# The maximum of v read by thirds, a last store from another tile, and a new load time in the planner

## The chip, the cores and the metric

The kernel runs on one core of one Trainium2 chip. The metric is the device time of one execution in microseconds. Each kernel is built once and run several times; the time before is the median of three runs. A profile is one further execution, recorded by the hardware profiler.

The engines are named as in the profile: PE is TensorE (matmuls), PEld its loads of the stationary operand, DVE is VectorE, ACT is ScalarE, POOL is GpSimd, SP is SyncE, on whose queue this kernel issues every DMA.

## The reference

Linear attention over 8 batches of 8 heads with 576 rows of 64, and then a feed-forward layer over the 4608 rows of 512 that come out of it:

```python
def phi(x):                                   # x: q or k
    proj = einsum('bhsd,df->bhsf', x, w_phi)  # 64 -> 128
    proj = proj - max(abs(proj), axis=-1, keepdims=True)
    return concatenate([exp(proj), exp(-proj)], axis=-1)
kv = einsum('bhsf,bhsd->bhfd', phi(k), v)
z = sum(phi(k), axis=2)
num = einsum('bhsf,bhfd->bhsd', phi(q), kv)
den = einsum('bhsf,bhf->bhs', phi(q), z)[..., None] + 1e-6
x = (num / den).transpose(0, 2, 1, 3).reshape(4608, 512)
h = x @ w_in                                  # 512 -> 2048
g = h / (1 + exp(-1.702 * h))
out = g @ w_out                               # 2048 -> 512
```

Inputs and output are float32; the two weights of the layer come as 64-bit floats.

## The kernel before

**Precision.** Most matmuls work on pairs of float16 or float32r numbers: a value is split into a high part and a low part, and three products are summed for one float32 product. To be split into float16, a tensor is scaled by a power of two that is taken from its maximum. For the attention's result that maximum is bounded by the maximum of |v| over a pair of batches (`SB = 2`). `batch_max(sb, stage)` (line 589) finds it for pair `sb`: it loads the whole of v of one batch into `stage`, 128 partitions by 2304 elements, reduces it on DVE to one column, does the same for the second batch, and `allmax` (line 533) carries the result across the partitions with a transpose and a matmul on PE. The four pairs are called pair 1 to pair 4 here (`sb` 0 to 3). The maximum gives `iv`, with which v is split, and `usc` and `osc`, with which the layer's intermediate values are scaled.

**Stages.** `load_weights` and `split_weights` bring the layer's weights in, turn them from 64-bit into float32 and split them; they share the first quarter of the span with the attention of the first two batches. From then on two kinds of work run interleaved: `attention(b)` for batches 2 to 7, and `moe_chunk`, the layer for 256 or 384 rows at a time. For each of 16 blocks `j` of 128 features `moe_chunk` runs a group of matmuls into one of two `hb` banks of PSUM; ACT takes the tanh of it (`th`), DVE makes `g` from `th` and the bank, which frees the bank; ACT and DVE split `g` into `gh` and `gl`; and matmuls over `gh` and `gl` add to the three `ab` banks. When a chunk is through, ACT copies each `ab` bank into one of two `osb` tiles, and `store` writes it out in one or two DMAs.

**Tiles.** A result of the attention for one batch lies in an `x` tile, of which there are three. `batch_max` uses as `stage` the `x` tile that its pair's first batch is going to fill. The weights that come in and `kept`, a partial result of the first two chunks, use `x` tiles too. `tl` is one tile of 128 partitions by 768 elements, in which `tail_load` (line 639) puts the last 64 rows of k, q and v of a batch. `e` is a pool of two tiles for exponentials.

**What sets the order.** Nothing is issued as it is written. A `Recorder` records every operation with its engine, tiles and dependencies; `R.part(v0, v1)` gives the operations behind it a due time between v0 and v1, in units of chunks of 384 rows. `schedule` (line 237) then plays a model of the engines: `cost` (line 192) gives each operation a duration, and of the operations that could start at an engine's free time the one with the earliest due time is taken; one that is due late is taken early if its engine has nothing else. A tile is handed to its next user when its last one is done. All operations are emitted in that order, each engine works through its own list in order, and semaphores keep the dependencies. So a changed duration, due time or tile changes the order on every engine. In the profile all these instructions carry one line, that of the recording, L346, and are told apart by tile names.

In `cost` a matmul has a load and a streaming time; a matmul may start, in the model, when the previous one has started and the load has passed:

```python
load = ap[1].shape[-1] / (1.2 if wide else 2.4)
...
return (load, n / 2.4 + (14.0 if wide else 3.0), 1)
```

`batch_max` of a pair is due at `u - VB`, where `u` is the due time of the pair's first batch (pair 1 has a due time of its own).

Of the kernel before, what the change touches and what calls it, by code (L numbers as in the profile page):

```python
# [8 lines left out]
F32 = mybir.dt.float32  # L9
# [101 lines left out]
class Recorder:  # L111
# [80 lines left out]
    def cost(eng, meth, args, kw):  # L192
# [9 lines left out]
        if eng == "tensor":  # L202

            wide = mybir.dt.size(ap[1].dtype) == 4
            load = ap[1].shape[-1] / (1.2 if wide else 2.4)
            if meth == "transpose":
                return (load, max(n, 32) / 2.4 * (2 if n > 64 else 1) + 1.5, 1)
            if ap[2].dtype == F32:
                m = 1.3 if n < 200 else 1.0
                return (m * load, m * n / 1.2, 2)  # L210
            return (load, n / 2.4 + (14.0 if wide else 3.0), 1)
# [138 lines left out]
def attn_moe_kernel(ctx, tc, q, k, v, w_phi, w_in, w_out, out):  # L350
# [10 lines left out]
    MAIN = 512  # L361
    TX = 0
    NEX = 6
# [43 lines left out]
    def new(nm):  # L407
        return R.tile(pools[nm])

    def small(n, nm="sm"):  # L410
        return R.tile(pools[nm])[:, 0:n]
# [176 lines left out]

    def batch_max(sb, stage):
        vmx = small(2, "sc")  # L590
        for i in range(2):
            R.sync.dma_start(
                stage,
                v[2 * sb + i].rearrange("h s d -> (h s d)").rearrange("(p n) -> p n", p=P),
            )
            R.vector.tensor_reduce(
                vmx[:, i : i + 1], stage, AX.X, ALU.max, apply_absolute_value=True
            )
        allmax(vg[:, sb : sb + 1], vmx)
        R.vector.reciprocal(iv[:, sb : sb + 1], vg[:, sb : sb + 1])  # L600
# [252 lines left out]

    def attn_unit(b, hp, nat, tail, nt, x32, x16, exact, bank):
        kq, vn = nat
# [133 lines left out]
        )  # L989
        j0 = 0  # L990
        xj = xf.rearrange("p j a d -> p j (a d)")
        if exact:
            tp = psa()
            for j in range(j0, 4):
                R.tensor.transpose(tp[:, j * P : (j + 1) * P], xj[:, j], ident)
            x, tp = slice(0, MAIN - j0 * P), tp[:, j0 * P :]
            R.scalar.copy(xh[:, hp, x], tp)
            R.vector.tensor_sub(xl[:, hp, x], tp, xh[:, hp, x])
        else:
# [67 lines left out]

    def moe_first(x32):

        acc = [R.tile(ab, whole=True) for m in range(TX // P)]  # L1070
        for j in range(NJ):
            R.part(-9.0 + 0.2 * j, -9.0 + 0.2 * (j + 1))
            load_weights(j)
            R.part(-5.825 + 0.54 * j, -5.825 + 0.54 * (j + 1), ("vector", "scalar"))
            hps = R.tile(hb, whole=True)[:, 0:TX]
            for ct in range(NCT):
                R.tensor.matmul(
                    hps,
                    wbuf[:, 2 * j + 1, ct * P : (ct + 1) * P],
                    x32[:, ct],  # L1080
                    start=ct == 0,
                    stop=ct == NCT - 1,
                )
            th = new("th")[:, 0:TX]
            R.scalar.activation(th, hps, AF.Tanh, scale=0.851)
            g = new("g")[:, 0:TX]
            R.vector.scalar_tensor_tensor(g, th, 1.0, hps, ALU.add, ALU.mult)
            for m in range(TX // P):
                R.tensor.matmul(
                    acc[m],  # L1090
                    g[:, m * P : (m + 1) * P],
                    wbuf[:, 2 * j + 2],
                    start=j == 0,
                    stop=j == NJ - 1,
                )
        for m in range(TX // P):
            osb = new("osb")
            R.scalar.activation(osb, acc[m], AF.Copy, scale=0.5)
            store(0, m * P, osb)

    def moe_chunk(sb, c0, n, part_=None):
# [35 lines left out]
        for m in range(n // P):  # L1137
            row = kept[:, c0 // P + m] if part_ is not None else None
            if part_ == 0:
                R.scalar.activation(row, acc[m], AF.Copy, scale=osf[:, 0:1])  # L1140
                continue
            osb = new("osb")
            if part_ is None:
# [8 lines left out]
    xs = {}  # L1152
    VB = 0.1
    V1 = (-1.1375, 0.5)
# [9 lines left out]
    def attention(b):  # L1164
        sb = b // SB
        u = v_att(4 * b)
        xt = new("x").rearrange("p t c s -> p (t c s)")
        x32, x16 = None, xt
        if b == 0 and TX:
            x32 = xt[:, 0 : 2 * NCT * TX].bitcast(F32).rearrange("p (c s) -> p c s", c=NCT)  # L1170
            x16 = xt[:, 2 * NCT * TX :]
        x16 = x16.rearrange("p (t c s) -> p t c s", t=2, c=NCT)
        xh, xl = x16[:, 0], x16[:, 1]
        xs[b] = (xh, xl)
        if b == 0:
            R.part(u + 0.002, u + 0.002)
            load_phi()
        R.part(u + 0.003 if b == 0 else u - 0.01, u)
        tl = tail_load(b)
# [5 lines left out]
        for hp in range(NHP):  # L1185
            if hp == 0 and b % SB == 0:
                z = u - VB if b else u + 0.975
                R.part(z, z)
                batch_max(sb, xt.bitcast(F32))
                if b == 0:  # L1190
                    R.vector.tensor_scalar(csx, vg[:, 0:1], 2.0**-13, None, ALU.mult)
            i = 4 * b + hp
# [5 lines left out]
            nat = attn_load(b, hp)  # L1198
            attn_unit(b, hp, nat, tail, nt, x32, x16, i < NEX, bank)
        return x32  # L1200

# [68 lines left out]
```

## Time and profile before

| | us |
|---|---|
| median of 3 runs | 1125.96 (1124.01 to 1129.14) |
| the profiled execution | 1123.7 |
| its span, first to last instruction | 1121.8 |
| PE busy in it | 1078.0 (96%) |
| PEld busy | 775.0 (69%) |
| DVE busy | 862.5 (77%) |
| ACT busy | 713.7 (64%) |
| POOL busy | 228.2 (20%) |

A busy PE is not PE at its peak, since the ends of matmuls are modelled and matmuls overlap; a PE that is idle is idle. The mean granted clock of TensorE over the span is 0.992 of full speed. Beside the page's shares the views that matter here are the busy time by stretch, the waits, and the timeline of PE and DVE around single waits.

### The profile page before, as it was taken

To read this page: it belongs to the slowest core of one execution; us is meant where nothing else is said; L and a number is where in the kernel's file an instruction comes from. 1 tells how busy PE (TensorE), PEld (TensorE's weight loads), DVE (VectorE), ACT (ScalarE), POOL (GpSimd) and SP (SyncE) were. 2 spreads that over 40 slices of the span, in tenths; PEclk is the share of its full clock that TensorE was granted. 3 is DMA by queue.
4 is the path that set the end of the run, shared out by engine and by line. 5 is a ranking of instruction groups with operands and counts; after the bars stand their busy time and mean duration, and the time that the engine had idled before them with its cause. 6 is when DMAs were issued, how large, how long until landed. Compare 5 with 4: busy or idle time off the path is not lost.

```text
span 1121.8 us, 22818 instructions
## 1 busy us (share of the span) xinstructions
PE 1078.0 (96%) x8915; PEld 775.0 (69%) x8915; DVE 862.5 (77%) x1763; ACT 713.7 (64%) x1483; POOL 228.2 (20%) x282
## 2 busy tenths in 40 slices
PE   5997999998999999999999999999999999999997
PEld 3664677876777757678876766678876667577653
DVE  5899988997799998887789988898879776422322
ACT  4577786874597876576677676586577666432423
POOL 6445101111123211230132211221122211100000
PEclk9998999999999999999999999999999999999999
DMA  8855113344143262242242252242223230000101
GB/s 271 267 183 143 57 38 78 73 97 144 23 94 77 61 179 48 53 97 56 48 100 57 58 162 57 61 105 58 48 67 58 42 63 11 11 29 2 29 1 29
DMA packets 172524, 87.80 MB, mean 78 GB/s; under 512 B 140032, under 2 KB 164736, under 8 KB 171392
## 3 DMA queue, kind: packets, MB, share of 16 engines
q1 hardware_dynamic: 172416, 86.34, 30.7%
q8 instruction: 70, 1.15, 0.4%
q14 instruction: 38, 0.31, 0.1%
HBM read 54.59 MB, written 9.44 MB: 57 GB/s over the span
## 4 chain that ended last, share of the span: by engine, by line
PE 77%; DVE 12%; ACT 5%; DMA 3%; issue 2%; SPq 1%; POOL 0%; ACTq 0%; DVEq 0%; POOLq 0%
PE ab L346 30%; PE hb L346 28%; PE at L346 19%; DMA xT<-xs 2%; DVE el L346 2%; DVE sm L346 2%; DVE t L346 1%; ACT e L346 1%; DVE gl L346 1%; DVE g L346 1%; DVE ks L346 1%; ACT eh L346 1%; DVE sc L346 1%; DVE vs L346 1%; DVE xs L346 1%
## 5 line engine op out<-in xcount | busy, mean ns | idle before, releaser
L346 PE MATMUL hb<-x,wbuf 128*128 128x192 f16 (+3 forms) x3264 | 479.8, 281 | 6.2 <-DVE g L346 5.9
L346 PE MATMUL ab<-wbuf,gh 128*128 128x512 f16 x1152 | 345.2, 382 | 0.2
L346 PEld LDWEIGHTS <-wbuf 128*128 128x128 f16 x3264 | 280.4, 98 | 80.5 <-issue 8.4
L346 ACT ACTIVATE th<-hb,usc 128x384 f32<-128x384 f32 (+1 forms) x208 | 115.8, 557 | 136.8 <-PE hb L346 126.6
L346 PE MATMUL ab<-wbuf,gl 128*128 128x512 f16 x576 | 198.8, 382 | 1.1 <-DVE gl L346 1.0
L346 DVE SCALAR_TENSOR_TENSOR g<-th,hb 128x384 f32<-128x384 f32 (+1 forms) x208 | 107.3, 517 | 105.6 <-ACT th L346 103.5
L346 PEld LDWEIGHTS <-gh 128*128 128x128 f16 x1152 | 108.9, 98 | 80.3 <-ACT gh L346 2.2
L346 DVE TENSOR_TENSOR el<-e,eh 128x512 f16<-128x512 f32 (+1 forms) x210 | 145.9, 708 | 18.8 <-PE at L346 9.3
L346 DVE SCALAR_TENSOR_TENSOR gl<-g,al,gh 128x384 f16<-128x384 f32 (+1 forms) x176 | 111.5, 635 | 37.2 <-ACT gh L346 30.5
L346 ACT ACTIVATE gh<-g,al 128x384 f16<-128x384 f32 (+1 forms) x176 | 106.9, 609 | 50.9 <-DVE g L346 50.2
L346 POOL TENSOR_TENSOR xf<-nf,rc 128x512 f32<-128x512 f32 x28 | 31.3, 1118 | 422.1 <-DVE rc L346 309.6
L346 DVE TENSOR_REDUCE sm<-at 128x4 f32<-128x512 f32 x126 | 86.1, 683 | 21.3 <-PE at L346 20.6
L346 PE MATMUL at<-ph,xT 128*128 128x128 f16 x944 | 98.7, 222 | 0.3
L346 ACT ACTIVATE e<-at 128x512 f32<-128x512 f32 x144 | 85.7, 604 | 20.7 <-PE at L346 19.3
L346 ACT ACTIVATE e<-t 128x512 f32<-128x512 f32 x144 | 89.4, 637 | 5.5 <-DVE t L346 3.7
L346 PEld LDWEIGHTS <-gl 128*128 128x128 f16 x576 | 54.6, 98 | 50.4 <-DVE gl L346 7.2
L346 DVE SCALAR_TENSOR_TENSOR t<-at,ks,sm 128x512 f32<-128x512 f32 x118 | 87.8, 744 | 1.2
L346 PE MATMUL at<-kzs,eh 128*128 128x132 f32 x216 | 79.8, 376 | 0.0
L346 PE MATMUL at<-vs,eh 128*128 128x132 f32 x208 | 79.5, 382 | 0.0
L346 PEld LDWEIGHTS <-xT 128*128 128x128 f16 x944 | 67.1, 99 | 13.9 <-issue 0.5
L346 PE MATMUL at<-kzs,el 128*128 128x66 f32 (+1 forms) x212 | 73.3, 351 | 0.0
L346 PE MATMUL at<-vs,el 128*128 128x66 f32 x208 | 73.3, 352 | 0.0
(195 smaller groups left out, 1926.4 us busy)
## 6 DMA issues: line engine op xcount, KB each, us to landing
x<-in_v_dram SPq DMA_DIRECT2D x8, 1152.0 KB, 6.4
vn<-in_v_dram SPq DMA_DIRECT2D x64, 128.0 KB, 2.8
kq<-in_k_dram SPq DMA_DIRECT2D x32, 256.0 KB, 3.1
kq<-in_q_dram SPq DMA_DIRECT2D x32, 256.0 KB, 3.0
x<-in_moe_w_in_dram SPq DMA_DIRECT2D x10, 512.0 KB, 5.4
x<-in_moe_w_out_dram SPq DMA_DIRECT2D x10, 512.0 KB, 5.2
out_dram<-osb SPq DMA_DIRECT2D x40, 128.0 KB, 2.6
out_dram<-osb SPq DMA_DIRECT2D x16, 256.0 KB, 2.4
```

Of the source, the lines that this page charges most:

```text
L346: f(*[g(a) for a in o.args], **{k: g(a) for k, a in o.kw.items()})
```

## The change

- `batch_max` for pairs 2 to 4 reads each batch in three loads of 768 elements per partition into the `tl` tile and reduces each third to a column of its own; `allmax` then reduces six columns in place of two. Pair 1 still uses its `x` tile.
- It is recorded ahead of `tail_load`, so its thirds come before the pair's first tail in the one `tl` tile; it no longer holds an `x` tile; `VB` goes from 0.1 to 0.5, which makes it due earlier.
- The last block of output that the kernel copies goes into an `e` tile and not into an `osb` tile.
- In `cost` the load of a 16-bit operand is counted at 4.6 columns per ns in place of 2.4: 28 ns for 128 columns in place of 53.
- `moe_first`, `TX`, `x32` and `j0` are removed; with `TX = 0` none of them did anything.

```diff
-            load = ap[1].shape[-1] / (1.2 if wide else 2.4)
+            load = ap[1].shape[-1] / (1.2 if wide else 4.6)
...
-    def batch_max(sb, stage):
-        vmx = small(2, "sc")
-        for i in range(2):
-            R.sync.dma_start(
-                stage,
-                v[2 * sb + i].rearrange("h s d -> (h s d)").rearrange("(p n) -> p n", p=P),
-            )
+    def batch_max(sb, stage=None):
+        n = 1 if stage is not None else 3
+        vmx = small(SB * n, "sc")
+        for i in range(SB * n):
+            t = stage if n == 1 else new("tl").rearrange("p i s d -> p (i s d)")
+            vr = v[SB * sb + i // n].rearrange("h s d -> (h s d)").rearrange(
+                "(p a n) -> p a n", p=P, a=n
+            )
+            R.sync.dma_start(t, vr[:, i % n])
             R.vector.tensor_reduce(
-                vmx[:, i : i + 1], stage, AX.X, ALU.max, apply_absolute_value=True
+                vmx[:, i : i + 1], t, AX.X, ALU.max, apply_absolute_value=True
             )
...
-            osb = new("osb")
+            if c0 + n == SB * S and sb == B // SB - 1 and m == n // P - 1:
+                osb = new("e")[:, 0:DM]
+            else:
+                osb = new("osb")
...
-    VB = 0.1
+    VB = 0.5
...
+        if b % SB == 0:
+            z = u - VB if b else u + 0.975
+            R.part(z, z)
+            batch_max(sb, None if b else xt.bitcast(F32)[:, 0 : H * S * D // P])
+            if b == 0:
+                R.vector.tensor_scalar(csx, vg[:, 0:1], 2.0**-13, None, ALU.mult)
         R.part(u + 0.003 if b == 0 else u - 0.01, u)
         tl = tail_load(b)
...
         for hp in range(NHP):
-            if hp == 0 and b % SB == 0:
-                z = u - VB if b else u + 0.975
-                R.part(z, z)
-                batch_max(sb, xt.bitcast(F32))
-                if b == 0:
-                    R.vector.tensor_scalar(csx, vg[:, 0:1], 2.0**-13, None, ALU.mult)
```

The order that comes of it, at three places.

DVE at the maximum of pair 3. In the kernel before, the reduction of a whole batch (`sc` from `x`) stands directly ahead of the `g` of two groups:

```order
L346 TENSOR_SCALAR ks_78<-ks_83,phg_163 128x2
L346 TENSOR_REDUCE sc_134<-x_113 128x1
L346 SCALAR_TENSOR_TENSOR g_117<-th_115,hb_65 128x384
L346 TENSOR_TENSOR el_144<-e_93,eh_141 128x512
L346 SCALAR_TENSOR_TENSOR g_118<-th_116,hb_64 128x384
```

In the changed kernel the first two thirds of this pair (`sc` from `tl`) stand so:

```order
L346 TENSOR_REDUCE sc_134<-tl_88 128x1
L346 SCALAR_TENSOR_TENSOR t_90<-at_62,ks_76,sm_126 128x512
L346 SCALAR_TENSOR_TENSOR xs_73<-kq_70,ks_77,xs_73 128x8x64
L346 TENSOR_SCALAR ks_86<-ks_86 128x2
L346 RECIPROCAL ks_81<-ks_86 128x2
L346 TENSOR_SCALAR ks_79<-ks_86,phg_163 128x2
L346 TENSOR_TENSOR el_144<-e_93,eh_142 128x512
L346 SCALAR_TENSOR_TENSOR g_117<-th_115,hb_65 128x384
L346 TENSOR_REDUCE sc_134<-tl_88 128x1
```

One reduction of 2304 elements has become three of 768, with seven other instructions between the first two of them.

SP at the same maximum. Before, the two loads of whole batches (`x` from v) have transposes and stores between them:

```order
L346 DMA x_113<-in_v_dram 128x2304
L346 DMA_TRANSPOSE xT_74<-xs_72 128x8x128
L346 DMA out_dram<-osb_123 64x512 x2
L346 DMA out_dram<-osb_124 64x512 x2
L346 DMA_TRANSPOSE xT_75<-xs_73 128x8x128
L346 DMA x_113<-in_v_dram 128x2304
```

Now:

```order
L346 DMA tl_88<-in_v_dram 128x768
L346 DMA_TRANSPOSE xT_75<-xs_73 128x8x128
L346 DMA tl_88<-in_v_dram 128x768 x3
L346 DMA_TRANSPOSE xT_75<-xs_72 128x8x128
L346 DMA_TRANSPOSE xT_74<-xs_73 128x8x128
L346 DMA tl_88<-in_v_dram 128x768
L346 DMA_TRANSPOSE x_114<-xo_111 128x4x128 x2
L346 DMA kq_70<-in_k_dram 128x2x256
L346 DMA kq_70<-in_q_dram 128x2x256
L346 DMA tl_88<-in_v_dram 128x768
```

Two loads have become six, three of them in a row, and two transposes of `xs` stand behind these three.

ACT at the end of the program, before (`ab` banks copied into `osb` tiles 124, 123 and 124 again):

```order
L346 ACTIVATE th_116<-hb_64,usc_176 128x384
L346 ACTIVATE gh_120<-g_118,al_172 128x384
L346 ACTIVATE osb_124<-ab_66,osc_177 128x512
L346 ACTIVATE osb_123<-ab_68,osc_177 128x512
L346 ACTIVATE osb_124<-ab_67,osc_177 128x512
```

and now:

```order
L346 ACTIVATE th_116<-hb_64,usc_176 128x384
L346 ACTIVATE gh_120<-g_118,al_172 128x384
L346 ACTIVATE osb_124<-ab_66,osc_177 128x512
L346 ACTIVATE osb_123<-ab_68,osc_177 128x512
L346 ACTIVATE e_93<-ab_67,osc_177 128x512
```

The last one writes a tile that no store reads.

## Rows read from the trace of the kernel before

**Rows 1.** The page, its first part: busy us, share of the span, instructions.
```profile
PE 1078.0 (96%) x8915; PEld 775.0 (69%) x8915; DVE 862.5 (77%) x1763; ACT 713.7 (64%) x1483; POOL 228.2 (20%) x282
```

**Rows 2.** Busy time by stretch: stretch, length, each engine, clock, DMA share, GB/s.
```profile
116.00:250.00 134.00, 132.86 (x1095) 98.00 (x1094) 120.83 (x272) 103.84 (x228) 18.89 (x24) 1.00 0.27 61
116.00:1114.00 998.00, 983.54 (x8364) 710.73 (x8362) 766.97 (x1589) 640.20 (x1342) 164.87 (x216) 1.00 0.27 62
490.00:500.00 10.00, 8.06 (x82) 7.54 (x81) 7.83 (x19) 5.87 (x13) 0.07 (x1) 0.83 0.22 54
```

**Rows 3.** Waits: who for whom, us in total, times, longest us.
```profile
PE hb L346 <- DVE g L346: 5.9, 6, 1.8
...
DVE sc L346 <- DMA x<-in_v_dram: 4.2, 3, 1.8
```

**Rows 4.** Instructions on tile sc: count, ns min/median/max, first and last start.
```profile
L346 DVE TENSOR_REDUCE sc<-x x8: 2536/2549/2553, 30.0 to 671.4; 128x1 f32<-128x2304 f32 x8
...
L346 DVE TENSOR_REDUCE sc<-sc x4: 99/143/148, 57.2 to 674.1; 128x1 f32<-128x2 f32 x4
```

**Rows 5.** Timeline, pair 2: start, us, engine, instruction, [idle before it <-releaser].
```profile
260.61 2.55 DVE L346 TENSOR_REDUCE sc<-x 128x1 f32<-128x2304 f32 x1 [1.82 <-DMA x<-in_v_dram]
263.08 0.74 DVE L346 SCALAR_TENSOR_TENSOR g<-th,hb 128x256 f32<-128x256 f32 x2
...
263.55 1.00 PE L346 MATMUL hb<-x,wbuf 128*128 128x64 f16 x18 [1.85 <-DVE g L346]
...
277.10 1.58 DVE L346 SCALAR_TENSOR_TENSOR vts<-tl,iv,vt 64x256 fp32r<-64x256 f32 x2
278.72 0.75 DVE L346 SCALAR_TENSOR_TENSOR g<-th,hb 128x256 f32<-128x256 f32 x2
...
279.19 0.39 PE L346 MATMUL hb<-x,wbuf 128*128 128x64 f16 x8 [0.92 <-DVE g L346]
```

**Rows 6.** Timeline, pairs 3 and 4.
```profile
404.27 2.55 DVE L346 TENSOR_REDUCE sc<-x 128x1 f32<-128x2304 f32 x1 [0.79 <-DMA x<-in_v_dram]
...
407.34 0.97 PE L346 MATMUL hb<-x,wbuf 128*128 128x384 f16 x5 [1.59 <-DVE g L346]
...
415.03 2.54 DVE L346 TENSOR_REDUCE sc<-x 128x1 f32<-128x2304 f32 x1
...
418.09 0.97 PE L346 MATMUL hb<-x,wbuf 128*128 128x384 f16 x5 [0.73 <-DVE g L346]
...
671.42 2.55 DVE L346 TENSOR_REDUCE sc<-x 128x1 f32<-128x2304 f32 x1 [1.58 <-DMA x<-in_v_dram]
...
674.39 0.27 PE L346 MATMUL at<-ident,sc 128*1 128x128 f32 x1 [1.19 <-DVE sc L346]
```

**Rows 7.** DMA issues of the page: count, KB each, median us to landing.
```profile
x<-in_v_dram SPq DMA_DIRECT2D x8, 1152.0 KB, 6.4
...
kq<-in_k_dram SPq DMA_DIRECT2D x32, 256.0 KB, 3.1
...
x<-in_moe_w_in_dram SPq DMA_DIRECT2D x10, 512.0 KB, 5.4
x<-in_moe_w_out_dram SPq DMA_DIRECT2D x10, 512.0 KB, 5.2
```

**Rows 8.** Matmuls of 64 columns: timeline; group by shape (busy us, mean ns, idle before).
```profile
250.20 0.51 PE L346 MATMUL hb<-x,wbuf 128*128 128x64 f16 x12
...
L346 PE MATMUL hb<-x,wbuf 128*128 128x64 f16 x192 | 9.4, 193 | 3.1 <-DVE g L346 3.0
```

**Rows 9.** Timeline of the end: PE, ACT and SP.
```profile
1113.95 0.38 PE L346 MATMUL ab<-wbuf,gl 128*128 128x512 f16 x1
...
1113.51 1.27 ACT L346 ACTIVATE osb<-ab,osc 128x512 f32<-128x512 f32 x2 [1.35 <-PE ab L346]
...
1116.02 0.59 SPq L346 DMA_DIRECT2D out_dram<-osb  x1
...
1117.31 0.69 ACT L346 ACTIVATE osb<-ab,osc 128x512 f32<-128x512 f32 x1 [2.54 <-DMA out_dram<-osb]
```

More of the change, by code (lines that the diff above doesn't have):

```diff
@@ L361, in attn_moe_kernel @@
     MAIN = 512
-    TX = 0
     NEX = 6
@@ L852, in across, with attn_unit @@
             R.scalar.copy(dst, tp.rearrange("p (j d) -> p j d", j=4))
-    def attn_unit(b, hp, nat, tail, nt, x32, x16, exact, bank):
+    def attn_unit(b, hp, nat, tail, nt, x16, exact, bank):
         kq, vn = nat
@@ L989, in attn_unit @@
         )
-        j0 = 0
         xj = xf.rearrange("p j a d -> p j (a d)")
@@ L993, in attn_unit @@
             tp = psa()
-            for j in range(j0, 4):
+            for j in range(4):
                 R.tensor.transpose(tp[:, j * P : (j + 1) * P], xj[:, j], ident)
-            x, tp = slice(0, MAIN - j0 * P), tp[:, j0 * P :]
-            R.scalar.copy(xh[:, hp, x], tp)
-            R.vector.tensor_sub(xl[:, hp, x], tp, xh[:, hp, x])
+            R.scalar.copy(xh[:, hp, 0:MAIN], tp)
+            R.vector.tensor_sub(xl[:, hp, 0:MAIN], tp, xh[:, hp, 0:MAIN])
         else:
@@ L1065, in store @@
             p0 += n
[L1068 to L1082, printed above, removed]
-                )
[L1084 to L1096, printed above, removed]
-            osb = new("osb")
-            R.scalar.activation(osb, acc[m], AF.Copy, scale=0.5)
-            store(0, m * P, osb)
     def moe_chunk(sb, c0, n, part_=None):
@@ L1141, in moe_chunk @@
                 continue
-            osb = new("osb")
+            if c0 + n == SB * S and sb == B // SB - 1 and m == n // P - 1:
+                osb = new("e")[:, 0:DM]
+            else:
+                osb = new("osb")
             if part_ is None:
@@ L1167, in attention @@
         xt = new("x").rearrange("p t c s -> p (t c s)")
[L1168 to L1172, printed above, removed]
+        x16 = xt.rearrange("p (t c s) -> p t c s", t=2, c=NCT)
         xh, xl = x16[:, 0], x16[:, 1]
@@ L1198, in attention @@
             nat = attn_load(b, hp)
-            attn_unit(b, hp, nat, tail, nt, x32, x16, i < NEX, bank)
-        return x32
+            attn_unit(b, hp, nat, tail, nt, x16, i < NEX, bank)
     attention(0)
```

## The prediction

> **What bounds the kernel now.** I read the page's busy shares first, then busy time by stretch, then the waits, then the timeline around the longest waits of TensorE. TensorE is busy for 96% of the span [rows 1], and from 116 to 1114 us it is busy 983.54 of 998 us [rows 2]. So in nine tenths of the span the time is set by how many matmuls stand there, which the change leaves alone, and a change of order can win only the 14.5 us that TensorE idles there, the end behind the last matmul, and what a low clock costs. VectorE (DVE) is the engine that TensorE waits for: 120.83 busy of 134 us between 116 and 250 [rows 2], and "hb <- DVE g" is the longest kind of wait of TensorE in the steady part, 5.9 us in 6 waits [rows 3].
>
> These waits have one origin more often than any other. The maximum of v over a pair of batches reads one whole batch per reduction: 8 reductions of 128x2304, 2.55 us each [rows 4], two in a row per pair. DVE takes its instructions in order, so the `g` that frees a bank of `hb` stands behind them. At 260.61 DVE starts such a reduction, after 1.82 us of waiting for the load; `g` follows at 263.08, and TensorE has idled 1.85 us when it gets the bank at 263.55 [rows 5]. After the second one, `g` at 278.72 stands behind the scaling of v by this maximum (vts), and TensorE idles 0.92 us [rows 5]. The next pair costs 1.59 and 0.73 us at 407.34 and 418.09, the last one 1.19 us at 674.39, where a matmul takes the reduction's own result [rows 6]. Together 1.85 + 0.92 + 1.59 + 0.73 + 1.19 = 6.3 of the 14.5 us. The other 8.2 us are many waits without a common cause. The first pair's two reductions stay as they are.
>
> **Part 1: maxima by thirds, sooner.** For pairs 2 to 4 the change takes out 6 loads of 1152 KB and 6 reductions of 2.55 us, and puts in 18 loads of 384 KB and 18 reductions of 768 elements. One takes 0.85 (a third of 2.55) to 0.94 us (with the 0.14 us of a reduction of two elements [rows 4] not shared out); I take 0.9. DVE work goes from 15.3 to 16.2 us: +0.9 us, on an engine with idle time. The gain is in the size of the piece. The slack between DVE and TensorE can be read off the waits: a delay of 1.82 + 2.55 cost 1.85 (slack 2.5), 0.79 + 2.55 cost 1.59 (1.75), 2.55 alone cost 0.73 (1.8) [rows 5, 6]. Against the smallest slack, 1.75 us, a third of 0.9 us alone costs TensorE nothing.
>
> The price: all thirds use the one `tl` tile. The next load waits on SyncE's queue (SP) until DVE has reduced the one before, and what is queued behind it there waits too: loads of k and q, transposes xT and x. A load of 384 KB does not occur before. 256 KB land in 3.1 us, 512 KB in 5.2 to 5.4, 1152 KB in 6.4 [rows 7]; the line from 256 to 1152 KB gives 3.5 (estimate), the 512 KB rows, taken while the weights came in, bound it at 5.3. I take 3.5, since 256 KB is nearest and the weights are in by then. Between the ends of the 15 successions the order leaves DVE other work, which I summed with the durations of the trace: 3.6, 3.8, 1.9, 9.6, 4.8 us in pair 2; 3.4, 4.3, 2.7, 17.9, 10.5 in pair 3; 3.1, 20, 5.9, 5.0, 8.5 in pair 4. Where it is under 3.5 us, DVE waits for the load: 1.6, 0.1, 0.8 and 0.4 us. Each with its 0.9 us, less the slack of 1.75: 0.8 us of TensorE once, else nothing. At a landing of 5.3 the same working gives 8.8 us. So part 1 is 0.8 - 6.3 = -5.5 us, with ends at -6.3 and +2.5. Of the 1.19 us at 674.39, which is the chain behind the last reduction and not its length, I leave 1 us standing: -4.5 us. If a stall goes, next late is `g` behind other DVE work, which is where the 8.2 us come from.
>
> Here a rule speaks against the change. The rows say 6.4 us for a whole batch and 3 x 3.5 = 10.5 us for its thirds. The Trainium skill (DMA: Bandwidth & Descriptors, "Measured (HBM→SBUF, 128 partitions, SWDGE, issued from GpSimd)") advises loads of 1 MiB or more, and its section "Anatomy of one DMA — SWDGE (gpsimd) path" gives 2.0 us plus bytes at 436 KB per us: 2.9 us for a third, 4.7 for the whole, an estimate by that page. By it the whole sum below would be about -7.9 in place of -7.3, since thirds would be awaited less; the trace's 6.4 us for 1152 KB is longer than the page's, and the trace decides.
>
> **Part 2: where they are put.** With VB 0.5, and no `x` tile to wait for, pair 2's reductions move from 260 us to the stretch that held 139 to 168 us, where the weights are split. DVE idles 13.2 us between 116 and 250 [rows 2], which covers 6 x 0.9 = 5.4 us; without that cover they would cost 5.4. The scaling by the maximum then no longer stands in front of `g` as at 277.10.
>
> **Part 3: last block from an `e` tile.** The last activation waits 2.54 us for its `osb` tile, whose store is under way [rows 9]. With its own tile it starts behind the two before it (they end at 1114.78, the last matmul at 1114.33) and ends near 1115.5. But SP issues the stores one after the other, and the fourth ends at 1116.61 [rows 9], so the fifth starts there, near 1116.7, and not at 1118.0, where the last activation ends now. -1.3 us, and nothing can take it back; ends -1.0 and -2.5 (the whole wait).
>
> **Part 4: the shorter float16 load.** No instruction changes; the planner counts 28 ns in place of 53 for a load of 128 columns. Twelve matmuls of 64 columns, each with its own load, take 0.51 us, the last one's 0.19 among it: 29 ns apart [rows 8]. So the new figure is the true one, and the plan's time for DVE against TensorE comes nearer the chip. Its effect is a new order everywhere after 98 us. One thing can be counted: the TensorE work between the end of a group in a bank of `hb` and the next group in this bank (spaced as in the trace). It must cover tanh and `g`. It is under 1.5 us at 7 places before, at 2 now. The unattributed 8.2 us, and a stretch of 10 us at a mean granted clock of 0.83 between 490 and 500 [rows 2], so 1.7 us lost to the lower level of 1.2 GHz behind two waits of TensorE, are what this can act on. I take -1.5 us, ends -6 and +5: a new order also makes new waits.
>
> **Sum.** -4.5 - 1.3 - 1.5 = -7.3 us on the profiled execution's 1123.7 (span 1121.8): 1116.4. The median of the runs shown, 1125.96, lies 2.3 above that execution, so the forecast for a median is 1118.7.
>
> **Rivals.** (a) The order is better throughout: nearly all of 6.3 us, 5 of the 8.2 and the 1.7 of the clock go: -5.5 - 1.3 - 6.7 = -13.5, 1112.5. For it: 7 places against 2. Against: pair 2's attention work is drawn forward into a stretch where DVE is already 90% busy. (b) The wait is exchanged: DVE awaits thirds as it now awaits whole batches (4.2 us in 3 waits [rows 3]), part 1 and part 4 are nothing, the end's 1.3 us stay: 1124.7. (c) Slower: SP's queue. In pairs 3 and 4 three thirds stand in a row with xT transposes directly behind. If a third lands in 5.3 us and not 3.5, each moves the transposes by 1.8 us, 5.4 per pair, 10.8 in all, with part 1 at +2.5 and the end at -1.3: +12, 1138. It decides from a landing of about 4.2 us on. Against it: 256 KB land in 3.1. (d) The plan's new figure is too short and its order denser than the chip can follow: half of the 8.2 us comes on top, +4.1 - 4.5 - 1.3 = -1.7, 1124.3; the 29 ns speak against it. Beside it stands the Trainium skill (TensorE: Matmul & The Clock Gate, "LDWEIGHTS (loading the stationary operand)"): columns / 1.2 ns, 107 ns for 128 columns; by that rule (d) would be the likeliest, but the trace does not agree with it.
>
> **How the numbers follow.** About 0.5% (5.6 us) is what a measurement here can tell from no change: faster is under 1120.3, slower over 1131.6. The forecast has 0.58, with its own range of 1114 to 1123: 0.44 of it faster, 0.14 the same. (a) 0.13, faster. (b) 0.13 and (d) 0.06, the same. (c) 0.10, slower. That is 0.57, 0.33 and 0.10. The range reaches from 1110 (all lower ends: -6.3 - 2 - 6, and a little for the runs) to 1128, which takes in (b), (d) and the milder part of (c).
>
> **What would show it.** Right: 18 reductions of about 0.9 us and none of 2.55 behind 60 us; thirds landing in 3 to 4 us; "hb <- DVE g" at a third of its 5.9 us; the last activation without a wait. Wrong: DVE waits for `tl` loads above 5 us in sum; TensorE waits for xT behind them; TensorE idle above 14 us between 116 us and the last matmul, or a new stretch at the lower clock.

## Result and profile after

The changed kernel takes 1111.42 us, median of 6 runs (1108.15 to 1112.23); the kernel before, run beside it, 1126.11 (1124.01 to 1129.14). The ratio is 0.9862, with a 95% interval of [0.9841, 0.9882]: 14.7 us faster. The direction was forecast and the size was not: 7.3 us were expected. The profiled execution took 1108.6 us, its span is 1106.8 (before 1121.8).

The page of the changed kernel, busy time first, then three of the costliest groups and the loads of thirds:

```profile
PE 1071.5 (97%) x8915; PEld 772.9 (70%) x8915; DVE 857.5 (77%) x1775; ACT 713.4 (64%) x1483; POOL 225.9 (20%) x282
...
L346 PE MATMUL hb<-x,wbuf 128*128 128x192 f16 (+3 forms) x3264 | 480.4, 281 | 1.4 <-DVE g L346 1.3
L346 PE MATMUL ab<-wbuf,gh 128*128 128x512 f16 x1152 | 342.0, 382 | 3.0 <-ACT gh L346 3.0
...
tl<-in_v_dram SPq DMA_DIRECT2D x18, 384.0 KB, 3.2
```

Against [rows 1], TensorE does the same 8915 matmuls in 6.5 us less busy time. The rest of the span, in which it isn't busy, goes from 43.8 to 35.3 us. So of the 15.0 us, 8.5 are idle time and 6.5 are time that the page of before called busy. The same by stretch, changed kernel, columns as in [rows 2]:

```profile
116.00:250.00 134.00, 133.96 (x1113) 99.61 (x1111) 125.73 (x284) 104.29 (x231) 24.47 (x33) 1.00 0.35 80
116.00:1099.00 983.00, 976.58 (x8364) 708.38 (x8363) 762.40 (x1600) 639.89 (x1341) 158.68 (x215) 1.00 0.29 63
490.00:500.00 10.00, 9.96 (x98) 7.87 (x97) 9.97 (x20) 6.19 (x14) 1.49 (x3) 1.00 0.43 110
```

From 116 us on, as many matmuls as in [rows 2], 8364, stand in 983 us and not in 998: 8.0 us less idle (14.46 before, 6.42 now), 7.0 us less busy. Between 490 and 500 us the granted clock is at its upper level (2.4 GHz) throughout, where it was 0.83 on average. The 1.7 us that the lower level cost there [rows 2] can be part of the 7.0; the other 5.3 us have another cause.

The waits of TensorE in the changed kernel, and the thirds of the maximum as DVE works through them:

```profile
PE ab L346 <- ACT gh L346: 3.0, 6, 0.8
...
PE hb L346 <- DVE g L346: 1.3, 3, 0.8
```

```profile
L346 DVE TENSOR_REDUCE sc<-tl x18: 900/944/954, 140.8 to 625.7; 128x1 f32<-128x768 f32 x18
```

"hb <- DVE g" is down from 5.9 us in 6 waits [rows 3] to 1.3 in 3. A wait of `ab` for ACT's `gh` has come up instead, 3.0 us. Every sign that the prediction named for being right is there (18 reductions near 0.9 us, thirds landing in 3.2 us, this wait below a third, the last activation without a wait), and none of those for being wrong. The signs didn't tell that the sum was wrong; the experiments did.

### The profile page after: what moved, and what is told of

The parts are those of the page before. It is cut to its first block, busy times and chain, and to the rows that moved or that the text cites. A ratio compares the mean times of both kernels' runs of the same rounds, so it can differ in the third digit from the quotient of the medians.

```text
span 1106.8 us, 22847 instructions
## 1 busy us (share of the span) xinstructions
PE 1071.5 (97%) x8915; PEld 772.9 (70%) x8915; DVE 857.5 (77%) x1775; ACT 713.4 (64%) x1483; POOL 225.9 (20%) x282
## 4 chain that ended last, share of the span: by engine, by line
PE 86%; DVE 5%; ACT 4%; DMA 2%; issue 1%; SPq 1%; POOL 0%; ACTq 0%; DVEq 0%; POOLq 0%
PE ab L346 33%; PE hb L346 31%; PE at L346 21%; DMA xT<-xs 2%; ACT e L346 1%; SPq L346 1%; DVE sm L346 1%; DVE ks L346 1%; ACT eh L346 0%; DVE gl L346 0%; DMA kq<-in_q_dram 0%; DVE t L346 0%; DVE wbuf L346 0%; DVE vs L346 0%; DVE g L346 0%
## 5 line engine op out<-in xcount | busy, mean ns | idle before, releaser
L346 PE MATMUL ab<-wbuf,gl 128*128 128x512 f16 x576 | 195.2, 382 | 0.4 <-DVE gl L346 0.3
L346 PE MATMUL at<-ph,xT 128*128 128x128 f16 x944 | 105.4, 222 | 0.5 <-DVE t L346 0.5
```

The source lines that it names most:

```text
L346: f(*[g(a) for a in o.args], **{k: g(a) for k, a in o.kw.items()})
```

## Experiments: the parts, one by one

All runs of an experiment stand against runs of the kernel before on the same chip, in 3 rounds (5 for the last pair); the ratio is to these. Their medians lay between 1124.1 and 1126.1 us over all sessions.

**The `e` tile alone.**

```diff
-            osb = new("osb")
+            if c0 + n == SB * S and sb == B // SB - 1 and m == n // P - 1:
+                osb = new("e")[:, 0:DM]
+            else:
+                osb = new("osb")
```

> The kernel before with one edit: the last copied block of output goes into an e tile. If the end is a term of its own, -1.3 us (ratio 0.9988), the last activation no longer waits 2.54 us, and the rest of the order stays as it was. If the end's gain is taken back elsewhere (the stores behind each other on SP), under -0.5 us.

Measured 1123.63, ratio 0.9990 [0.9974, 1.0006]. The last activation no longer waits, as [rows 9] let one expect (ACT at the end, this kernel):

```profile
1115.28 1.27 ACT L346 ACTIVATE osb<-ab,osc 128x512 f32<-128x512 f32 x2 [1.35 <-PE ab L346]
1116.43 0.69 ACT L346 ACTIVATE e<-ab,osc 128x512 f32<-128x512 f32 x1
```

Every instruction of TensorE and of DVE stands in the same order as before, so this is no new order. The size agrees with -1.3 us, but the interval holds no change too. The profiles are sharper than the runs: from the end of the last matmul to the end of the span it is 7.5 us before (1114.33 [rows 9] to 1121.8) and 6.3 us here (1116.10 to 1122.4).

```profile
1115.72 0.38 PE L346 MATMUL ab<-wbuf,gl 128*128 128x512 f16 x1
```

In all six kernels of this study with the `e` tile this stretch is 6.3 or 6.4 us, in the fourteen without it 7.5 to 7.7. So the tile is worth some 1.2 us at the end, though the times of the runs scatter too much to show it.

**The load figure alone.**

```diff
-            load = ap[1].shape[-1] / (1.2 if wide else 2.4)
+            load = ap[1].shape[-1] / (1.2 if wide else 4.6)
```

> The kernel before with one edit: the planner counts the load of a 16-bit operand at 4.6 columns per ns. Theory L (a plan nearer to the chip makes a denser order of matmuls): TensorE's busy time falls by most of the 6.5 us by which it fell in the changed kernel (1078.0 to 1071.5), and the time by 6 us or more (ratio under 0.995); the 2.55 us reductions stay, and with them some of the waits of hb for g. Rival B (the gain is that of the thirds): within 2 us of the kernel before, TensorE busy about 1077.

Measured 1109.85, ratio 0.9868 [0.9853, 0.9884]: this one number gives all that the whole change gives. Its page and its longest stretch:

```profile
PE 1071.4 (97%) x8915; PEld 772.5 (70%) x8915; DVE 858.2 (77%) x1763; ACT 715.6 (65%) x1483; POOL 228.5 (21%) x282
```

```profile
116.00:1099.00 983.00, 975.90 (x8363) 707.65 (x8362) 761.73 (x1588) 641.75 (x1341) 164.00 (x215) 1.00 0.28 63
```

The busy times of TensorE, of its loads and of DVE are those of the changed kernel within 0.8 us, in both rows. TensorE's has fallen by 6.6 us, as theory L of the expectation had it. And yet the reductions of whole batches are still there. DVE and PE at the first one of pair 2 in this kernel:

```profile
259.75 2.54 DVE L346 TENSOR_REDUCE sc<-x 128x1 f32<-128x2304 f32 x1
262.21 0.48 DVE L346 SCALAR_TENSOR_TENSOR gl<-g,al,gh 128x256 f16<-128x256 f32 x1
262.61 0.41 DVE L346 SCALAR_TENSOR_TENSOR g<-th,hb 128x256 f32<-128x256 f32 x1
```

```profile
259.82 1.17 PE L346 MATMUL hb<-x,wbuf 128*128 128x192 f16 x20
260.83 1.03 PE L346 MATMUL ab<-wbuf,gh 128*128 128x512 f16 x4
261.70 1.07 PE L346 MATMUL hb<-x,wbuf 128*128 128x192 f16 x11
262.75 0.60 PE L346 MATMUL ab<-wbuf,gl 128*128 128x512 f16 x2
```

It is the same piece, and `g` still stands behind it, now with a `gl` between. DVE doesn't wait for the load here, where it waited 1.82 us before [rows 5], and TensorE has other work at hand for the whole length of the piece and doesn't idle, where it idled 1.85 us before. Not every such wait goes. At the first reduction of pair 3 TensorE idles 0.47 us for `g`, and not 1.59, but also 1.04 us for ACT's `osb` just ahead; and the wait behind the scaling of v, 0.92 us before, is still there:

```profile
278.72 0.59 PE L346 MATMUL hb<-x,wbuf 128*128 128x64 f16 x13 [1.09 <-DVE g L346]
...
405.66 0.59 PE L346 MATMUL ab<-wbuf,gh 128*128 128x512 f16 x2 [1.04 <-ACT osb L346]
...
407.26 0.97 PE L346 MATMUL hb<-x,wbuf 128*128 128x384 f16 x5 [0.47 <-DVE g L346]
```

**The thirds and their place alone** (the changed kernel with these two parts undone).

```diff
-            load = ap[1].shape[-1] / (1.2 if wide else 4.6)
+            load = ap[1].shape[-1] / (1.2 if wide else 2.4)
...
-            if c0 + n == SB * S and sb == B // SB - 1 and m == n // P - 1:
-                osb = new("e")[:, 0:DM]
-            else:
-                osb = new("osb")
+            osb = new("osb")
```

> The changed kernel without the new load time and without the e tile: maxima by thirds, sooner, alone. Rival B (the gain is that of the thirds): -8 us or more against the kernel before, idle time of TensorE down by about 6 us. Theory L: -4 to -5 us, idle time down, but busy time of TensorE near 1078.

Measured 1119.04, ratio 0.9946 [0.9928, 0.9964]: -5.9, between the two theories of the expectation. TensorE's busy time is 1075.0 us, 3 us less than before, so it falls without the new load figure too.

**The block alone, order kept.** The planner's order is that of the kernel before; when it is issued, the six reductions of pairs 2 to 4 read 768 of their 2304 elements.

```diff
+            if o.meth == "tensor_reduce" and args[1].shape[-1] == 2304:
+                whole += 1
+                if whole > 2:
+                    args[1] = args[1][:, 0:768]
```

> The kernel before with its order kept instruction for instruction; only the six reductions of whole batches for pairs 2 to 4 read a third of their elements (768 in place of 2304), so the maximum is taken over a third of v, and DVE is blocked about 0.95 us in place of 2.55 each time. If the block ahead of g is what costs (the prediction's part 1), the waits of 1.85, 0.23, 1.59 and 0.73 us shrink to under 0.5 us in all: -4 to -5 us. If these waits only cover others that stand behind them, under -2 us.

Measured 1122.24, ratio 0.9973 [0.9960, 0.9987]: -2.7, between the two forecasts. The wait for `g` falls nearly as far as in the changed kernel (L352 is the recording's line here):

```profile
PE hb L352 <- DVE g L352: 1.8, 4, 0.9
```

So 4.1 us of "hb <- DVE g" go with the length of the reductions, and the time falls by 2.7 us (1124.95 to 1122.24, by the interval 1.5 to 4.5). The block is real. But the parts do not add: -1.3, -15.1 and -5.9 alone, and not -22.3 but -14.7 together. The two that make a new order largely take away the same waits: "hb <- DVE g" is 1.8 us with the load figure alone, 1.9 with the thirds alone and 1.3 with both, from 5.9.

## Experiments: what a number of the planner does

Three theories were put against each other. N: the plan now has the narrow float16 matmuls at their true 29 ns [rows 8]. S: the plan has TensorE faster, by whatever route, and so puts the work of the other engines ahead of it. C: any new order lands somewhere by chance. The experiments change two numbers of `cost` only, the load of a 16-bit operand in columns per ns (2.4) and the constant that is added to every 16-bit matmul (3.0 ns).

```diff
-            load = ap[1].shape[-1] / (1.2 if wide else 2.4)
+            load = ap[1].shape[-1] / (1.2 if wide else 10.0)
```

> The kernel before, with the 16-bit load at 10 columns per ns (13 ns) in the planner. A matmul of 64 columns streams 30 ns in the plan, so the load is hidden from 4.6 on and the planned time hardly differs from that with 4.6; only a few choices between operations come out differently. Theory N (what counts is that the plan has the narrow float16 matmuls at their true 30 ns): 1110, within 2 of the load alone. Theory S (what counts is that the plan has TensorE faster by any route, so the work of the other engines is drawn ahead): the same, 1110. Theory C (any changed order lands somewhere by chance): anywhere from 1108 to 1125, and a difference of 5 or more from 1109.9 would speak for it.

Measured 1109.58, ratio 0.9855 [0.9826, 0.9885].

```diff
-            load = ap[1].shape[-1] / (1.2 if wide else 2.4)
+            load = ap[1].shape[-1] / (1.2 if wide else 3.4)
```

> The kernel before, with the load at 3.4 columns per ns: 38 ns for a narrow matmul in the plan, against 53 before and 30 on the chip, so 15 of 23 ns of the error are gone. Theories N and S: about two thirds of the 15 us that the load alone gave, 1115 (1112 to 1118). Theory C: anywhere from 1108 to 1125.

Measured 1114.81, ratio 0.9901 [0.9878, 0.9923].

```diff
-            return (load, n / 2.4 + (14.0 if wide else 3.0), 1)
+            return (load, n / 2.4 + (14.0 if wide else 0.5), 1)
```

> The kernel before, load as it was (2.4), and the constant that the plan adds to each 16-bit matmul's streaming 0.5 ns in place of 3.0. The plan of TensorE is some 20 us shorter, as with the load at 4.6 (26 us), but the narrow matmuls are still at 53 ns in it. Theory N: no gain, 1125 (1122 to 1127). Theory S: most of the gain, 1113 (1110 to 1116). Theory C: anywhere from 1108 to 1125.

Measured 1113.96, ratio 0.9892 [0.9869, 0.9915]. Theory N had no gain here.

```diff
-            load = ap[1].shape[-1] / (1.2 if wide else 2.4)
+            load = ap[1].shape[-1] / (1.2 if wide else 4.6)
...
-            return (load, n / 2.4 + (14.0 if wide else 3.0), 1)
+            return (load, n / 2.4 + (14.0 if wide else 5.5), 1)
```

> The load at 4.6, and the constant of each 16-bit matmul at 5.5 ns in place of 3.0, so that the plan of TensorE is nearly as long as before (6 us shorter), with the narrow matmuls at their true time. Theory N: the gain stays, 1110 (1108 to 1113). Theory S: the gain goes, 1121 (1118 to 1125). Theory C: anywhere from 1108 to 1125.

Measured 1116.16, ratio 0.9911 [0.9887, 0.9935]: between N's 1110 and S's 1121. With f5 this speaks against N alone: a true figure for the narrow matmuls is neither needed for a gain nor enough to hold it.

Next, small steps against the direction of the change, to see whether the kernel before lies on a trend at all:

```diff
-            load = ap[1].shape[-1] / (1.2 if wide else 2.4)
+            load = ap[1].shape[-1] / (1.2 if wide else 2.3)
```

> The kernel before with the 16-bit load at 2.3 columns per ns in place of 2.4: narrow matmuls at 56 ns in the plan and not 53, a step against the direction of the change, by an eighth of it. Theories N and S (the time follows the plan's time of TensorE): 1125 + 2 = 1127 (1125 to 1129). Theory C (the order of the kernel before is one of its worse draws, and any disturbance of it lands near the middle of 1110 to 1125): 1116 (1110 to 1122).

Measured 1120.19, ratio 0.9958 [0.9943, 0.9973].

```diff
-            return (load, n / 2.4 + (14.0 if wide else 3.0), 1)
+            return (load, n / 2.4 + (14.0 if wide else 3.3), 1)
```

> The kernel before with the constant of each 16-bit matmul at 3.3 ns in place of 3.0, the load as it was: the plan of TensorE 2.5 us longer by its parts, again a small step against the direction of the change. Theories N and S: 1126 (1124 to 1128). Theory C: 1116 (1110 to 1122).

Measured 1118.21, ratio 0.9933 [0.9911, 0.9955].

```diff
-            return (load, n / 2.4 + (14.0 if wide else 3.0), 1)
+            return (load, n / 2.4 + (14.0 if wide else 2.7), 1)
```

> The kernel before with the constant at 2.7 in place of 3.0, the load as it was, a small step in the direction of the change. If the kernel before is a poor draw by 6 us: 1118 (1115 to 1121), as for 3.3 and for the load of 2.3. If it lies on the trend and the other two were lucky: 1124 (1122 to 1126).

Measured 1117.30, ratio 0.9928 [0.9910, 0.9947]. Three neighbours, on both sides, lie at 1117.3 to 1120.2, mean 1118.6, and the kernel before at 1125.0. It is a poor draw, by 6.4 us. Where the draw went, in the kernel with 3.3: the reductions first, then TensorE's wait, then the stretch.

```profile
L346 DVE TENSOR_REDUCE sc<-x x8: 2534/2542/2553, 29.8 to 667.0; 128x1 f32<-128x2304 f32 x8
```

```profile
PE hb L346 <- DVE g L346: 2.8, 5, 1.0
```

```profile
116.00:1110.00 994.00, 983.46 (x8378) 710.22 (x8376) 763.77 (x1589) 644.34 (x1344) 163.07 (x216) 1.00 0.28 62
```

The eight reductions are as long as in [rows 4]. TensorE's busy time is that of before (983.46 for 14 matmuls more), its idle time 10.5 and not 14.5 us. Of the 6.3 us of waits at the five places of [rows 5, 6] this kernel keeps 0.5, that with the load at 2.3 0.5, and that with 2.7 none; the load at 4.6 keeps 1.6. Those waits were for the most part a coincidence of that one order. Some new ones come in their place: 1.8 us at 489 us in the kernel with 3.3. The stretch at the lower clock near 490 us, 1.7 us before, is gone from all three neighbours too (1.00 between 490 and 500 us).

Then far steps, both ways:

```diff
-            load = ap[1].shape[-1] / (1.2 if wide else 2.4)
+            load = ap[1].shape[-1] / (1.2 if wide else 1.8)
```

> The kernel before with the load at 1.8 columns per ns: narrow matmuls at 71 ns in the plan, and other short ones (a stream of 128 columns, 56 ns) behind their load too. The plan of TensorE is 36 us longer. Theory S: the gain of 15 us for 26 us less, turned round, 1145 (1135 to 1150). Theory N: 42 ns of error per narrow matmul in place of 24: 1137 (1130 to 1145). Theory C: 1116 (1110 to 1122).

Measured 1140.97, ratio 1.0137 [1.0114, 1.0160].

```profile
PE 1090.2 (96%) x8915; PEld 774.4 (68%) x8915; DVE 862.0 (76%) x1763; ACT 715.9 (63%) x1483; POOL 227.2 (20%) x282
```

```profile
PE ab L346 <- ACT gh L346: 6.5, 13, 0.9
```

Theory C falls at this end: 22 us slower than the neighbours' mean, and TensorE waits 13 times for `gh`, 6.5 us. TensorE counts as busy 12 us longer for the same 8915 matmuls.

```diff
-            load = ap[1].shape[-1] / (1.2 if wide else 2.4)
+            load = ap[1].shape[-1] / (1.2 if wide else 4.6)
...
-            return (load, n / 2.4 + (14.0 if wide else 3.0), 1)
+            return (load, n / 2.4 + (14.0 if wide else 1.0), 1)
```

> The load at 4.6 and the constant at 1.0 in place of 3.0: the plan of TensorE 14 us shorter than with the load alone. Theory S: the other engines' work is drawn ahead still further, 1104 (1101 to 1107). Theory N: the load has given all there is, 1110, and a plan that is too short in its other matmuls costs a little: 1112 (1109 to 1116). Theory C: 1115 (1108 to 1122).

Measured 1107.89, ratio 0.9844 [0.9825, 0.9862]: 2 us below the load alone, in S's direction, though S had 6. The intervals of the two overlap, so the step itself is not shown. Its page:

```profile
PE 1069.4 (97%) x8915; PEld 772.3 (70%) x8915; DVE 857.7 (78%) x1763; ACT 717.3 (65%) x1483; POOL 227.9 (21%) x282
```

```diff
-            load = ap[1].shape[-1] / (1.2 if wide else 2.4)
+            load = ap[1].shape[-1] / (1.2 if wide else 4.6)
...
-            return (load, n / 2.4 + (14.0 if wide else 3.0), 1)
+            return (load, n / 2.4 + (14.0 if wide else -1.0), 1)
```

> The load at 4.6 and the constant at -1.0: each 16-bit matmul 2 ns shorter in the plan than with 1.0, some 14 us in all by its parts. Theory S as a straight trend: 1106 (1104 to 1108). If there is a best point near 1.0, where a plan that is too short sends TensorE's other work too early: 1110 (1108 to 1115).

Measured 1117.00, ratio 0.9928 [0.9913, 0.9944]. That is a step back of 9 us, and three waits within 30 us hold most of it (PE's timeline of this kernel):

```profile
246.54 0.59 PE L346 MATMUL hb<-x,wbuf 128*128 128x64 f16 x13 [1.10 <-DVE g L346]
...
253.01 0.58 PE L346 MATMUL at<-ii,zt 128*128 128x64 f16 x8 [3.57 <-DVE t L346]
...
273.84 0.76 PE L346 MATMUL hb<-x,wbuf 128*128 128x64 f16 x15 [2.43 <-DVE g L346]
```

1.10 + 3.57 + 2.43 = 7.1 us. Around the longest of them the granted clock fell, to 0.66 on average between 250 and 260 us, which is 3.4 us lost:

```profile
250.00:260.00 10.00, 6.31 (x50) 5.97 (x51) 7.97 (x21) 3.61 (x7) 0.84 (x2) 0.66 0.65 198
```

So this is either a second poor draw or the far side of a best point; without neighbours of it the two can't be told apart.

## Experiments: are the thirds needed?

The changed kernel with whole batches, as in the kernel before, at their old place (the load figure and the `e` tile on the kernel before):

```diff
-            load = ap[1].shape[-1] / (1.2 if wide else 2.4)
+            load = ap[1].shape[-1] / (1.2 if wide else 4.6)
...
-            osb = new("osb")
+            if c0 + n == SB * S and sb == B // SB - 1 and m == n // P - 1:
+                osb = new("e")[:, 0:DM]
+            else:
+                osb = new("osb")
```

> The changed kernel with whole batches, as before, in place of thirds, at their old place: the load of 4.6 and the e tile alone. If the thirds add nothing once the order is another: 1109.85 of the load alone less 1.3 for the tile, 1108.6 (1107 to 1110), 3 faster than the changed kernel's 1111.4. If they are still worth the 3 us of the shortened reductions: 1114 or more, slower than the changed kernel.

Measured 1109.88, ratio 0.9863 [0.9845, 0.9880]: what the load figure gives without the tile (1109.85), and what the changed kernel gives with thirds. With the constant at 1.0 on the changed kernel:

```diff
-            return (load, n / 2.4 + (14.0 if wide else 3.0), 1)
+            return (load, n / 2.4 + (14.0 if wide else 1.0), 1)
```

> The changed kernel with the constant of a 16-bit matmul at 1.0 ns in place of 3.0. Theory S (trend): 2 us less than the changed kernel, as the same step gave on the load alone (1109.85 to 1107.89): 1109.4 (1108 to 1111). If only chance is left at this end: 1106 to 1115, without a lean.

Measured 1107.89, ratio 0.9850 [0.9831, 0.9868]. And a last pair on one chip, in 5 rounds: the load figure, the constant at 1.0 and the `e` tile on the kernel before, and the changed kernel as it is.

```diff
-            load = ap[1].shape[-1] / (1.2 if wide else 2.4)
+            load = ap[1].shape[-1] / (1.2 if wide else 4.6)
...
-            return (load, n / 2.4 + (14.0 if wide else 3.0), 1)
+            return (load, n / 2.4 + (14.0 if wide else 1.0), 1)
...
-            osb = new("osb")
+            if c0 + n == SB * S and sb == B // SB - 1 and m == n // P - 1:
+                osb = new("e")[:, 0:DM]
+            else:
+                osb = new("osb")
```

> The kernel before with the load of 4.6, the constant at 1.0 and the e tile, whole batches as before. If thirds are not needed: 1107.9 of the same without the tile, less what the tile gives (0 to 1.3): 1107 (1105.5 to 1108.5), 3 to 4 below the changed kernel. If they are: 1111 or more.

> The changed kernel once more, beside the other on the same chip: 1111.4 (1109.5 to 1112.5) under every theory.

Measured 1107.16 (1105.89 to 1107.89), ratio 0.9843 [0.9820, 0.9865], and 1108.68 (1107.58 to 1109.29), ratio 0.9860 [0.9840, 0.9880]. The kernel without thirds is 1.5 us lower, but the runs overlap; and the changed kernel, 1111.4 in its first session, is 2.7 us lower in this one, outside what was expected. The kernel before is 2.1 us lower beside it, and the ratio is that of the first session (0.9860 and 0.9862). From 1107 to 1111 nothing here is told apart. What is shown is that the thirds add nothing that can be measured once the planner has the new load figure.

## Why the prediction was right and wrong

**What failed: how far the order reaches.** The step is the first one: "in nine tenths of the span the time is set by how many matmuls stand there, which the change leaves alone, and a change of order can win only the 14.5 us that TensorE idles there, the end behind the last matmul, and what a low clock costs". From 116 us on the number of matmuls was the same, 8364, and their busy time fell from 983.54 to 976.58 us; the low clock, which the prediction had counted, is at most 1.7 of these 7.0 us. Over the kernels of this study TensorE's busy time for the same 8915 matmuls runs from 1069.4 us (load 4.6, constant 1.0) to 1090.2 (load 1.8), at the same mean granted clock of 0.993. Busy time is no count of work that must be done. The Trainium skill (Perfetto Trace Analysis, "Identifying the Most-Contended Engine") says that matmul busy time is no good measure of how close a kernel is to its limit, since matmuls are pipelined, and advises the busy share of the weight loads, beside another measure, in its place. The traces agree: PEld runs only from 772.3 to 774.4 us in these two kernels, and from 771.9 to 777.7 over all.

How a wait can hide in busy time is seen in the rows above: a matmul of 512 columns is booked with 382 ns, but two of them in a row take 600 ns, so the second starts 218 ns after the first. A wait of up to some 160 ns behind such a matmul leaves no idle time in the profile. The start times in the traces show that this matters. If the distance of each matmul from the one ahead is held against what is usual for the same pair of shapes over all kernels here, then, from 116 us on, 18 of the 20.8 us between the two extremes are longer distances within the same pairs; the rest is another mix of pairs. Whether these are short waits or matmuls that run slower, the traces don't tell. For the 6.5 us of the changed kernel the split depends on what is taken for usual: 2 to 5 us are shorter distances.

**Part 4 was mis-sized by a factor of ten.** Forecast -1.5 us with ends of -6 and +5; alone it gave -15.1, outside both. I had costed it by the 8.2 us that were left over of the idle time, and had given the reductions' waits to part 1 alone. In fact the new order took 4.7 of those 6.3 us too, and the neighbours' orders took nearly all. By the mean of the neighbours the 15.1 us split into 6.4, which leaving this order is worth (1125.0 to 1118.6), and 8.7 on a trend (1118.6 to 1109.9). Against the kernel with 3.3 these 8.7 are busy time and idle time about alike: 1077.0 to 1071.4 us busy by the pages, 40.7 to 36.4 us of the span not busy, in the profiled executions.

The trend is shown in its direction. Here the kernels stand by how much longer or shorter the expectations put TensorE's plan (an eighth of 26 us for a load of 2.3, two thirds for 3.4; for 2.7 the step of 3.3 turned round). These figures are estimates and not measured:

| load, constant | plan, us | measured, us |
|---|---|---|
| 1.8, 3.0 | +36 | 1141.0 |
| 2.3, 3.0 | +3 | 1120.2 |
| 2.4, 3.3 | +2.5 | 1118.2 |
| 2.4, 3.0 (before) | 0 | 1125.0 |
| 2.4, 2.7 | -2.5 | 1117.3 |
| 4.6, 5.5 | -6 | 1116.2 |
| 3.4, 3.0 | -17 | 1114.8 |
| 2.4, 0.5 | -20 | 1114.0 |
| 4.6, 3.0 | -26 | 1109.9 |
| 10.0, 3.0 | -26 and hardly more | 1109.6 |
| 4.6, 1.0 | -40 | 1107.9 |
| 4.6, -1.0 | -54 | 1117.0 |

The times fall from row to row but for two, the kernel before and the one at -1.0. So the three neighbours lie on theory S's trend, and the kernel before stands some 7 us off it by chance; of the one at -1.0 it stays open. Single steps of 1 or 2 us in the table are within the scatter. Seen from the neighbours' mean and from the load alone, theory S has the sign of every far step but the one to -1.0; its sizes were off by 4 to 5 us in three of them. Theory N fails in both of its tests by this measure too: it had nothing for the constant of 0.5, which stands 4.6 us below the mean, and all of 8.7 us for a load of 4.6 with 5.5, which stands 2.4 below.

Why theory S holds in its direction is argued and not shown: a plan with a TensorE faster than the chip's has DVE and ACT further ahead, and on the chip that lead is slack. The idle time of DVE that ends with ACT's `th` falls along the faster half, from 103.5 us before to 92.2 at a load of 4.6 and 88.1 with the constant at 1.0 (the row of this last kernel):

```profile
DVE g L346 <- ACT th L346: 88.1, 40, 4.0
```

It is weak support: the changed kernel with the constant at 1.0 is as fast and has 97.5 us of it, and the slowest one, with the load at 1.8, has 100.7, less than before.

My argument that the figure is "the true one", and so the better one, is not what the runs show: a constant of 0.5, which is no truer, gave 11.6 us with the old load.

**Part 1: -4.5 forecast, -5.9 alone, nothing on top.** That the part alone comes near its forecast is luck: a disturbance without meaning gives 6.4. The mechanism was there, but smaller: the block itself is worth 2.7 us with the order kept. A third took 0.944 us (0.9 forecast) and landed in 3.2 us (3.5 forecast). By the fit of the Trainium skill (DMA: Bandwidth & Descriptors, "Anatomy of one DMA — SWDGE (gpsimd) path"), which is for loads that GpSimd issues, it would be 2.9, an estimate; the trace, with SP issuing, lies between the two. DVE waits for thirds three times, 0.93, 0.43 and 0.20 us (four times and 2.9 us were forecast); the longest:

```profile
145.53 0.95 DVE L346 TENSOR_REDUCE sc<-tl 128x1 f32<-128x768 f32 x1 [0.93 <-DMA tl<-in_v_dram]
```

What the sum missed is that -4.5 and part 4 were for the most part the same idle time, and so can't be added. One working in it is off: at a landing of 5.3 us the numbers shown give 8.4 us and not 8.8, which only moves an end that didn't come. **Part 2** cost nothing that can be seen, as forecast: DVE took 4.9 us more in 116 to 250 (125.73 against 120.83 in [rows 2]), and TensorE was busy 133.96 of 134. It wasn't tried apart from part 1. **Part 3** agrees in the profiles, 1.2 us behind the last matmul in every kernel with the `e` tile, and is too small for the times of the runs.

**The rivals.** (a), a better order throughout, 1112.5, comes nearest (1111.4), and its chance of 0.13 was too low. Its cause is the right one, but the nearness of its number is in part luck: it put the whole gain in idle time, the end and the clock, where 5.3 us or more of it were not. The stretch at the lower clock near 490 us went as it said. (b): DVE's waits for thirds, 1.6 us in all, didn't take the place of the 4.2 for whole batches. (c) needed landings above 4.2 us, and they were 3.2. (d), a plan too short for the chip to follow, didn't come at 4.6: shorter still, at a constant of 1.0, was no slower. Only at -1.0 did a loss come that could be its kind. That a float16 load is done in 28 ns, which the prediction took for shown, is more than its rows say: by its own record one lasts 98 ns, and those of the twelve matmuls of [rows 8] overlap.

## What to carry to other kernels

Where a planner sets the order, a number in it is worth what the new order is worth, and that is found by a handful of neighbours and not from the waits of one trace: run two or three meaningless disturbances first, to learn whether the present order is a poor draw (here 6 us of 15). Don't read an edit's own gain as the edit's before that: the thirds alone gave no more than such a disturbance. Waits that one can name in a trace may belong to the draw and not to the instruction beside them, so don't add what two edits win from the same idle time. And don't take the busy time of TensorE for fixed when the matmuls stay the same.

## What the runs showed of the hardware

The granted clock between 490 and 500 us, 0.83 before with two waits of TensorE ahead of the fall, was 1.00 in the changed kernel and with the load alone, where TensorE was busy 9.96 and 10.00 of those 10 us. The two waits of before:

```profile
491.18 0.39 PE L346 MATMUL at<-ii,zt 128*128 128x64 f16 x8 [1.48 <-DVE kf L346]
492.34 0.22 PE L346 MATMUL at<-v,eh 128*128 128x132 f16 x1 [0.77 <-ACT eqth L346]
```

With the constant at -1.0 it was 0.66 between 250 and 260 us, around a wait of 3.57 us, and with the `e` tile alone 0.66 between 490 and 500 us. TensorE's busy time for identical work differed by 20.8 us (2%) between the kernels of this study, the busy time of its weight loads in the same two by 2.1, and by 5.8 over all. The first depends on the order, the second much less. A float16 load of 128 columns lasts 98 ns by its record, and loads between matmuls of 64 columns start 29 ns apart (the eleven at the matmuls of [rows 8], and the group):

```profile
250.21 0.39 PEld L346 LDWEIGHTS <-wbuf 128*128 128x128 f16 x11 [0.18 <-issue]
...
L346 PEld LDWEIGHTS <-wbuf 128*128 128x128 f16 x3264 | 280.4, 98 | 80.5 <-issue 8.4
```
